# Sorted-block attention and a gated MLP on one core: six value loads issued in one row behind a softmax turn, one value product ahead of an output step, three copies on the other engine

## The chip, the cores and the metric

The kernel runs on one core of a Trainium2 chip. A core has five engines with instruction streams of their own: TensorE (PE in the profile; PEld is its weight load), VectorE (DVE), ScalarE (ACT), GpSimd (POOL) and SyncE (SP). Each runs its own stream in the order in which it was written, and they wait for each other, and for DMAs, on semaphores. The metric is the device time of one execution in microseconds (us); less is better.

## The reference

What is computed, cut to what matters (4 batches, 8 heads, 768 tokens, 64 wide; 8 blocks of 96 tokens; model width 512, inner width 2048):

```python
for _ in range(5):                          # P = sort_net, 8x8 for each head
    P = exp(P - max(P, -1)); P = P / (sum(P, -1) + 1e-9); P = P / (sum(P, -2) + 1e-9)
k_sorted = einsum('bhij,bhjcd->bhicd', P, k_b)      # blocks of keys mixed
v_sorted = einsum('bhij,bhjcd->bhicd', P, v_b)      # blocks of values mixed
scores = scale * q_b @ k_sorted^T                   # block by block, 96 x 96
attn = softmax(scores)
x = attn @ v_sorted                                  # as 3072 tokens x 512
h = x @ w_in                                         # 512 -> 2048
out = (h * cos(h)) @ w_out                           # 2048 -> 512
```

## The kernel before, in words

The work goes in eight **chunks** of 384 tokens: chunk n is half of the blocks (four of eight) of batch n // 2. Batches 0 and 1 are pair 0, batches 2 and 3 are pair 1. A chunk has four **turns** u, one for each block of 96 tokens:

- scores for all 8 heads on PE (`sc`), row maximum and subtraction on DVE (`qk_reduce`, lines 507 and 509), exp on ACT into one of three buffers `p_buf` (`expo`, line 587);
- the transpose of p, either by a DMA from SP's queue (line 607) or on PE (`p_ps`, line 854, with a copy `p_ev`);
- the **value product** (`av_products`, line 643), whose result DVE normalizes (`av_norm`, lines 654 and 656);
- the transpose of the normalized block into `xT`, by a DMA from SP's queue (line 662) or on PE with a copy out (`xp` and `xe`, lines 966 and 972).

The MLP of a chunk follows its attention: eight **up** steps (`uh`, line 915, with cosine on ACT, `uc`, and the product on DVE, `ug`), then three **output** blocks of 128 tokens, each in four quarters of four matmuls (`dn`, line 1012), copied out by `dc` (ACT for the first two blocks, DVE for the last) and stored.

Interleaved with it, the blocks of keys and values of the next pair are mixed: "key sort" (`kg`, `bt(('ks', ..))`, `sort_eight`) reads the tile `pair`, "value sort" (`vg`, `bt(('vs', ..))`) reads `vperm`. POOL makes `vperm` from `vbuf`, a half of the tile `kv`, by four large copies (`v_permute`, line 187). `vbuf` is loaded with pair 1's values by six loads (`load_pair`, line 101), each 128 rows by 1024 columns, from POOL's queue.

What sets the order is the code itself: the kernel turns the automatic schedule off, and the calls stand one behind the other by hand (lines 1028 to 1561). Each engine runs its share of them in that order. PSUM comes from two pools: `big` with three buffers of two banks (scores, value products, up steps, sorts), `acc` with two (output blocks, transposes). A new tile waits until the tile that had its buffer before has been read. The output tile of block (1,2) takes the `acc` buffer of block (1,1), so its first quarter, `dn(1, 2, 0)`, waits for the copy in `dc(1, 1)`.

Three more things matter for the change:

- `hold(t)` (line 615) is a tiny POOL copy out of a tile that a DMA writes. It has no use but to make POOL wait there: what POOL issues next is issued once that DMA has landed. `p_hold(n, u)` waits for the transposed p of turn u of chunk n.
- DMAs issued from POOL use eight semaphores in turn; each waits until the DMA eight places before it has landed. The eight loads of q for chunk 4 (`load_q(4)`) stand behind the six value loads, so the third to the eighth of them wait for the value loads, one each.
- SP's queue carries, in this order around the change: the two q transposes of chunk 3, the transposes of p of chunk 2 (turns 0, 1, 2), two stores, p of turn 0 of chunk 3, a store, the two q transposes of chunk 4, the two key swaps (`k_swap_b(0)`), p of turns 1 and 2 of chunk 3.

In the rows, L101 is `load_pair`, L138 is `load_q`, L158 `q_transpose_dma`, L265 and L267 the copy on ACT and on DVE.

Of the kernel before, what the change touches and what calls it, by code (L numbers as in the profile page):

```python
# [18 lines left out]
def kernel(  # L19
# [15 lines left out]
    nc = tc.nc  # L35
# [8 lines left out]
    CD = blk * D  # L44
# [24 lines left out]
    vbuf, kbuf = kv[:, :CD], kv[:, CD:]  # L69
# [24 lines left out]
    vin_d = v.rearrange("b h (j c) d -> b (h j) (c d)", j=nb)  # L94
# [4 lines left out]
    def load_pair(buf, src, lo, hi):  # L99

        nc.gpsimd.dma_start(  # L101
            out=buf[:, lo:hi], in_=src[2:4].rearrange("b r x -> (b r) x")[:, lo:hi])
# [158 lines left out]
    V, A = nc.vector, nc.scalar  # L261

    def copy_on(eng, dst, src):
        if eng is nc.scalar:
            eng.copy(dst, src)  # L265
        else:
            eng.tensor_copy(dst, src)  # L267
# [175 lines left out]
    def hold_keys():  # L443

        nc.gpsimd.tensor_copy(held[:], kT[1][:, 1, 0, :1])
# [70 lines left out]
    def by_half(n, u, sc):  # L516

        for h2 in range(H2):
            x = (u * H2 + h2) * blk
            for hp in range(2):  # L520
                rows = slice(hp * D, (hp + 1) * D)
                nc.tensor.matmul(  # L522
                    sc[:, hp, h2 * 128:h2 * 128 + blk], q_of(n, hp)[rows, x:x + 128],
                    keys_of(n, u, h2, hp)[rows], start=True, stop=True)

    def sort_eight(kind, z, ps):

        for t in range(8):
            for b in range(2):
                rows = slice(b * 64, (b + 1) * 64)  # L530
                if kind == "ks":
                    m, cols = 128, pair[rows, (z * 8 + t) * 2 * D:(z * 8 + t + 1) * 2 * D]
                else:
                    m, cols = 128, v_cols(z * 8 + t, True, 128)[rows]
                nc.tensor.matmul(
                    ps[:m, b, t * 2 * NB:(t + 1) * 2 * NB], cols,
                    bds[1][rows, b * H:(b + 1) * H].rearrange("p x i -> p (x i)"),
                    start=True, stop=True)
# [74 lines left out]
    def hold(t):  # L613

        nc.gpsimd.tensor_copy(held[:blk], t[:blk, 0, :1])

    def p_hold(n, u):
        hold(pT[n, u])
# [81 lines left out]
    def store(n, ts, o_s, eng=nc.sync):  # L700
        r0 = n * TC + ts * 128
        eng.dma_start(out=out[r0:r0 + 128, :], in_=o_s[:])
# [243 lines left out]
    def bt(*parts):  # L946
        for kind, *x in parts:
            o = big.tile([128, 2, 512], FP32, name=kind, tag="big")
            if kind == "sc":
                ps["q", x[0], x[1]] = o  # L950
                by_half(*x, o)
            else:
                ps["e", kind, x[0]] = o
                sort_eight(kind, x[0], o)

    def be(kind, z, eng):
        place_eight(kind, z, ps.pop(("e", kind, z)), eng)
# [11 lines left out]
    def xe(n, u, to, eng):  # L969
        hi = (u if to is None else to) + 1  # L970
        copy_on(eng, xT[n][:, :, u * blk:hi * blk],
                ps.pop(("t", n, u)).rearrange("p k i c -> p k (i c)"))
# [35 lines left out]
    def dn(n, ts, q):  # L1008
        if q == 0:
            out_ps[n, ts] = acc.tile([128, Dm], FP32, name="o", tag="acc")  # L1010
        for f in range(q * 4, q * 4 + 4):
            nc.tensor.matmul(  # L1012
                out_ps[n, ts][:], gt[n, q][:, f % 4, ts * 128:(ts + 1) * 128], w_out_t[:, f, :],
                start=(f == 0), stop=(f == FC - 1))

    def dc(n, ts, stores):
        if stores is None:
            z = (n % 2 * 3 + ts) * 2 * Dm
            o_s = vbuf[:, z:z + 2 * Dm].bitcast(FP32)
        else:  # L1020
            o_s = op.tile([128, Dm], FP32, name="o_s", tag="o_s")
        copy_on(V if ts == TC // 128 - 1 else A, o_s[:], out_ps.pop((n, ts))[:])
        if stores is None or stores == "held":
            kept[n, ts] = o_s
        else:
            store(n, ts, o_s, stores)
# [207 lines left out]
    zeros_between(3)  # L1234
    load_q(3)
    hold_keys()
    load_pair(vbuf, vin_d, 0 * CD // 6, 1 * CD // 6)
    load_pair(vbuf, vin_d, 1 * CD // 6, 2 * CD // 6)
    load_pair(vbuf, vin_d, 2 * CD // 6, 3 * CD // 6)
    uh(1, 0)  # L1240
    uc(1, 0)
    ug(1, 0)
# [61 lines left out]
    dn(1, 1, 1)  # L1304
    kg(16, *B)
    kge(16, A)
    dn(1, 1, 2)
    expo(2, 3, True)
    av_products(2, 0)
    av_norm(2, 0, True)  # L1310
    dn(1, 1, 3)
    dc(1, 1, nc.sync)
    bt(('sc', 3, 0), ('ks', 1, A))
    qr2(3, 0)
    be("ks", 1, A)
    p_hold(2, 2)
    load_pair(vbuf, vin_d, 3 * CD // 6, 4 * CD // 6)
    load_pair(vbuf, vin_d, 4 * CD // 6, 5 * CD // 6)
    load_pair(vbuf, vin_d, 5 * CD // 6, 6 * CD // 6)
# [12 lines left out]
    av_products(2, 2)  # L1332
    av_norm(2, 2, True)
    xp(2, 1, None, *B)
    xe(2, 1, None, V)
    av_products(2, 3)
    av_norm(2, 3, True)
    xp(2, 0, None, *C)
    xe(2, 0, None, V)
    dn(1, 2, 2)  # L1340
    kg(20, *B)
    kge(20, A)
# [61 lines left out]
    dn(2, 0, 3)  # L1404
    dc(2, 0, nc.sync)
    expo(3, 3)
    bt(('vs', 1, A), ('vs', 2, A))
    be("vs", 1, A)
    be("vs", 2, A)
    dn(2, 1, 0)  # L1410
    av_products(3, 0)
    av_norm(3, 0, False)
# [118 lines left out]
             None, mid={3: [(qk_av, 6, 1, 5, 2)]}, late=[(x_transpose, 5, 3, V, *B)])  # L1531
# [7 lines left out]
             None, mid={3: [(qk_av, 7, 1, 6, 2)]}, late=[(x_transpose, 6, 3, V, *B)])  # L1539
# [51 lines left out]
```

## Time and profile before

| what | value |
|---|---|
| time, median of 3 runs (lowest, highest) | 231.41 us (230.86, 231.49) |
| the profiled execution: time, span | 230.85 us, 229.1 us |
| TensorE clock granted | 1.0 |
| PE busy, of the span | 219.3 us (96%) |
| DVE, ACT, POOL busy | 171.8, 153.0, 95.2 us |
| PE busy from 69 to 84 us (15 us) | 14.69 us |
| PE busy from 96 to 110 us (14 us) | 13.48 us |

How to read the rows: a timeline row has the start in us from the span's start, the busy time in us, the engine, the line of the kernel, the operation, out<-in, the type, the count of instructions merged, and in brackets the idle time before them and what ended it. PE's matmuls are pipelined, so that rows of PE may overlap; the distance from start to start says more than their length. A DMA row ends with the count and the median time from issue to landing in us. The turns of chunk 2 lie between 70 and 84 us, those of chunk 3 between 97 and 110 us.

### The profile page before, as it was taken

To read this page: it belongs to the slowest core of one execution; us is meant where nothing else is said; L and a number is where in the kernel's file an instruction comes from. 1 tells how busy PE (TensorE), PEld (TensorE's weight loads), DVE (VectorE), ACT (ScalarE), POOL (GpSimd) and SP (SyncE) were. 2 spreads that over 40 slices of the span, in tenths; PEclk is the share of its full clock that TensorE was granted. 3 is DMA by queue.
4 is the path that set the end of the run, shared out by engine and by line. 5 is a ranking of instruction groups with operands and counts; after the bars stand their busy time and mean duration, and the time that the engine had idled before them with its cause. 6 is when DMAs were issued, how large, how long until landed. Compare 5 with 4: busy or idle time off the path is not lost.

```text
span 229.1 us, 5513 instructions
## 1 busy us (share of the span) xinstructions
PE 219.3 (96%) x2243; PEld 137.4 (60%) x2265; DVE 171.8 (75%) x297; ACT 153.0 (67%) x206; POOL 95.2 (42%) x120
## 2 busy tenths in 40 slices
PE   8688899999999999999999999999999999999994
PEld 3387798567665566645665456655655566555554
DVE  6779859987798768868589967987699769646700
ACT  5749865966989758897688466736674667716521
POOL 7999999299960288934517001800000000000000
PEclk9999999999999999999999999999999999999999
DMA  5999999996999699857979639953934440351012
GB/s 65 237 187 207 204 205 234 198 230 172 99 120 206 172 157 132 146 126 152 165 146 129 118 70 164 201 92 73 189 119 85 89 158 0 69 147 46 0 46 94
DMA packets 67833, 31.21 MB, mean 136 GB/s; under 512 B 56416, under 2 KB 63200, under 8 KB 67552
## 3 DMA queue, kind: packets, MB, share of 16 engines
q0 software_dynamic: 24048, 13.64, 43.4%
q1 hardware_dynamic: 43472, 17.02, 33.8%
q8 instruction: 18, 0.29, 0.6%
q10 hardware_dynamic: 288, 0.20, 0.3%
q14 instruction: 7, 0.06, 0.1%
HBM read 27.27 MB, written 6.29 MB: 147 GB/s over the span
## 4 chain that ended last, share of the span: by engine, by line
PE 80%; DVE 12%; ACT 4%; issue 2%; DMA 1%; ACTq 0%; DVEq 0%
PE h L687 18%; PE o L712 16%; PE h L915 14%; PE o L1012 11%; PE av L643 3%; DVE mx L839 3%; DVE s L843 3%; PE sc L457 3%; PE h L876 2%; PE ks L424 2%; PE o L897 2%; DVE gg L888 2%; PE o L1555 2%; ACT p_buf L587 1%; PE xps L966 1%
## 5 line engine op out<-in xcount | busy, mean ns | idle before, releaser
L687 PE MATMUL h<-xT,w_in_t 128*128 128x384 bf16 x256 | 43.2, 327 | 0.0
L691 ACT ACTIVATE c<-h,half_pi 128x768 f32<-128x768 f32 x32 | 28.8, 900 | 17.7 <-PE h L687 17.7
L712 PE MATMUL o<-w_out_t,gg 128*128 128x512 bf16 x169 | 39.9, 379 | 0.4
L695 DVE TENSOR_TENSOR gg<-c,h 128x768 bf16<-128x768 f32 x32 | 29.9, 950 | 11.6 <-ACT c L691 11.6
L915 PE MATMUL h<-xT,w_in_t 128*128 128x384 bf16 x192 | 35.2, 327 | 0.1
L687 PEld LDWEIGHTS <-w_in_t 128*128 128x128 bf16 x256 | 24.7, 98 | 16.2
L1012 PE MATMUL o<-w_out_t,gg 128*128 128x512 bf16 x134 | 33.7, 379 | 0.6 <-issue 0.3
L187 POOL COPY vperm<-kv 64x768 bf16<-64x768 bf16 (+2 forms) x12 | 28.4, 2417 | 4.8 <-DMA kv<-in_v_dram 4.8
L587 ACT ACTIVATE p_buf<-s 96x768 bf16<-96x768 f32 x32 | 26.6, 843 | 4.5 <-DVE s L509 4.0
L927 DVE TENSOR_TENSOR gg<-c,h 128x768 bf16<-128x768 f32 x24 | 22.7, 948 | 7.6 <-ACT c L921 7.6
L921 ACT ACTIVATE c<-h,half_pi 128x768 f32<-128x768 f32 x24 | 21.6, 900 | 8.3 <-PE h L915 7.4
L712 PEld LDWEIGHTS <-gg 128*128 128x128 bf16 x176 | 16.0, 98 | 16.5
L509 DVE TENSOR_TENSOR s<-sc,mx 96x384 f32<-96x384 f32 (+1 forms) x33 | 24.3, 735 | 1.6
L507 DVE TENSOR_REDUCE mx<-sc 96x4 f32<-96x384 f32 (+1 forms) x33 | 24.0, 728 | 0.4 <-PE sc L522 0.4
L915 PEld LDWEIGHTS <-w_in_t 128*128 128x128 bf16 x192 | 17.5, 98 | 9.9 <-DVE xT L267 0.3
L656 DVE TENSOR_TENSOR xn<-av,r 96x512 bf16<-96x512 f32 x32 | 22.0, 686 | 1.1
L1012 PEld LDWEIGHTS <-gg 128*128 128x128 bf16 x144 | 12.6, 97 | 12.0
L138 POOL DMA_DIRECT2D kv<-in_q_dram x24 | 16.0, 676 | 0.8 <-issue 0.8
L265 ACT COPY kv<-o 128x512 f32<-128x512 f32 (+2 forms) x10 | 5.2, 523 | 14.0 <-PE o L712 8.5
L265 ACT CAST kTs<-ks 128x512 bf16<-128x512 f32 (+1 forms) x17 | 10.4, 633 | 4.6 <-PE ks L424 4.6
L654 DVE RECIPROCAL r<-av 96x8 f32<-96x8 f32 x32 | 6.3, 197 | 7.3 <-PE av L643 7.1
L267 DVE COPY kv<-o 128x512 f32<-128x512 f32 (+1 forms) x5 | 3.1, 611 | 11.3 <-PE o L1555 8.5
(140 smaller groups left out, 335.9 us busy)
## 6 DMA issues: line engine op xcount, KB each, us to landing
out_dram<-kv SPq DMA_DIRECT2D x12, 256.0 KB, 2.7
out_dram<-o_s SPq DMA_DIRECT2D x10, 256.0 KB, 2.6
w_in_t<-in_moe_w_in_dram POOLq DMA_DIRECT2D x4, 512.0 KB, 12.0
w_out_t<-in_moe_w_out_dram POOLq DMA_DIRECT2D x4, 512.0 KB, 12.5
kv<-in_k_dram POOLq DMA_DIRECT2D x2, 768.0 KB, 10.3
kv<-in_v_dram POOLq DMA_DIRECT2D x2, 768.0 KB, 13.5
pair<-in_k_dram POOLq DMA_DIRECT2D x2, 768.0 KB, 13.2
kv<-in_v_dram POOLq DMA_DIRECT2D x6, 256.0 KB, 5.5
```

The source lines that it names most:

```text
L187: nc.gpsimd.tensor_copy(dst, src)
L507: nc.vector.reduce_max(mx[:], scv, axis=AX.X)
L509: nc.vector.tensor_tensor(s, scv, mx.to_broadcast(list(s.shape)), op=ALU.subtract)
L587: nc.scalar.activation(p[:, :, :blk], s_t.pop((n, u)).rearrange("p e h c -> p (e h) c"), AF.Exp, scale=scale)
L656: nc.vector.tensor_tensor(xn.rearrange("p h e d -> p e h d"), avv[:, :, :, :D], r.to_broadcast([blk, 2, H2, D]), op=ALU.mult)
L687: nc.tensor.matmul(h[:, f2, :w], w_in_t[:, kk, f * 128:(f + 1) * 128], xT[n][:, kk], start=(kk == 0), stop=(kk == KC - 1))
L691: nc.scalar.activation(c[:], h[:, :, :w], AF.Sin, bias=half_pi[:, 0:1])
L695: nc.vector.tensor_tensor(gt[n, fp // 2][:, f:f + 2], c[:], h[:, :, :w], op=ALU.mult)
L712: nc.tensor.matmul(o[:], gt[n, f // 4][:, f % 4, ts * 128:(ts + 1) * 128], w_out_t[:, f, :], start=(f == 0), stop=(f == FC - 1))
L915: nc.tensor.matmul(h[:, f2, :TC], w_in_t[:, kk, f * 128:(f + 1) * 128], xT[n][:, kk], start=(kk == 0), stop=(kk == KC - 1))
L927: nc.vector.tensor_tensor(gt[n, fp // 2][:, f:f + 2], ps.pop(("c", n, fp))[:], ps.pop(("h", n, fp))[:, :, :TC], op=ALU.mult)
L1012: nc.tensor.matmul(out_ps[n, ts][:], gt[n, q][:, f % 4, ts * 128:(ts + 1) * 128], w_out_t[:, f, :], start=(f == 0), stop=(f == FC - 1))
```

## The change

Three kinds of edits, no change to what is computed:

1. The first three of the six value loads leave their place behind `hold_keys()` and stand directly ahead of the other three. The wait ahead of these is now for p of turn 1 of chunk 2, and no longer for turn 2.
2. In the turns of chunk 2 the value product of turn 0 and its normalization stand ahead of the third quarter of output block (1,1), and the fourth quarter with its copy `dc(1, 1)` stands behind the scores of chunk 3, turn 0, and the key sort 1.
3. The copies `xe(2, 1)` and `xe(2, 0)` go from DVE to ACT; the eviction of value sort 2, `be("vs", 2, ..)`, goes from ACT to DVE.

```diff
     hold_keys()
-    load_pair(vbuf, vin_d, 0 * CD // 6, 1 * CD // 6)
-    load_pair(vbuf, vin_d, 1 * CD // 6, 2 * CD // 6)
-    load_pair(vbuf, vin_d, 2 * CD // 6, 3 * CD // 6)
     uh(1, 0)
...
     kge(16, A)
-    dn(1, 1, 2)
     expo(2, 3, True)
     av_products(2, 0)
     av_norm(2, 0, True)
-    dn(1, 1, 3)
-    dc(1, 1, nc.sync)
+    dn(1, 1, 2)
     bt(('sc', 3, 0), ('ks', 1, A))
     qr2(3, 0)
     be("ks", 1, A)
-    p_hold(2, 2)
+    dn(1, 1, 3)
+    dc(1, 1, nc.sync)
+    p_hold(2, 1)
+    load_pair(vbuf, vin_d, 0 * CD // 6, 1 * CD // 6)
+    load_pair(vbuf, vin_d, 1 * CD // 6, 2 * CD // 6)
+    load_pair(vbuf, vin_d, 2 * CD // 6, 3 * CD // 6)
     load_pair(vbuf, vin_d, 3 * CD // 6, 4 * CD // 6)
...
     xp(2, 1, None, *B)
-    xe(2, 1, None, V)
+    xe(2, 1, None, A)
...
     xp(2, 0, None, *C)
-    xe(2, 0, None, V)
+    xe(2, 0, None, A)
...
-    bt(('vs', 1, A), ('vs', 2, A))
+    bt(('vs', 1, A), ('vs', 2, V))
     be("vs", 1, A)
-    be("vs", 2, A)
+    be("vs", 2, V)
```

On POOL, from the q loads of chunk 3 on (`p_turned_138` is the transposed p of turn 2 of chunk 2, `p_turned_137` that of turn 1; L146 zeroes a part of `q_mem` for chunk 4):

```order
 L138 DMA kv<-in_q_dram 96x4x64 x8
 L445 CAST held<-kTs 128x1
-L101 DMA kv<-in_v_dram 128x1024 x3
 L146 MEMSET q_mem 96x16x64 x2
-L615 CAST held<-p_turned_138 96x1
-L101 DMA kv<-in_v_dram 128x1024 x3
+L615 CAST held<-p_turned_137 96x1
+L101 DMA kv<-in_v_dram 128x1024 x6
 L138 DMA q_mem<-in_q_dram 96x4x64 x8
 L187 COPY vperm<-kv 128x1536 x4
```

All six value loads now stand behind the wait for p of turn 1, and the q loads and the four permutes behind all six.

On ACT, in the turns of chunk 2, from the eviction of `kg(16)` to that of `kg(20)` (the `ks` of 8 columns is key sort 1, `o_s` is the copy of output block (1,1), `pps` the transposed p of turn 3):

```order
 L265 CAST kTs<-ks 128x2x2x32x4
 L587 ACTIVATE p_buf_105<-s 96x8x96
+L265 CAST kTs<-ks 128x2x2x32x8
 L265 COPY o_s<-o 128x512
-L265 CAST kTs<-ks 128x2x2x32x8
 L265 COPY p_turned_139<-pps 96x768
 L587 ACTIVATE p_buf_103<-s 96x8x96
+L265 COPY xT<-xps 128x4x96 x2
 L265 CAST kTs<-ks 128x2x2x32x4
```

The eviction of key sort 1 now stands ahead of the copy of the output block, and the two copies into `xT` are new on this engine.

## The prediction

> **What bounds the kernel now.** I read the page first, then the timeline of TensorE (PE) and of SyncE's DMA queue (SPq) from 63 to 84 us, then the waits, then the landing times of single DMAs.
>
> ```profile
> PE 219.3 (96%) x2243; PEld 137.4 (60%) x2265; DVE 171.8 (75%) x297; ACT 153.0 (67%) x206; POOL 95.2 (42%) x120
> ```
>
> PE bounds the kernel. An edit pays only where PE stands still, so the question is how much PE loses in the chunk-2 turns, and which wait ends last there. The timeline of PE (start, duration, line, count):
>
> ```profile
> 74.76 0.39 PE L424 MATMUL ks<-bd,pair 128*128 128x128 bf16 x4
> 74.98 1.03 PE L1012 MATMUL o<-w_out_t,gg 128*128 128x512 bf16 x4
> 76.01 0.42 PE L643 MATMUL av<-vS,p_turned 96*128 96x65 bf16 x8
> 76.27 1.03 PE L1012 MATMUL o<-w_out_t,gg 128*128 128x512 bf16 x4
> 77.23 0.34 PE L522 MATMUL sc<-kTs,q_turned 64*128 64x96 bf16 x8
> ...
> 77.74 0.42 PE L643 MATMUL av<-vS,p_turned 96*128 96x65 bf16 x8
> 77.99 0.50 PE L854 MATMUL pps<-ident,p_buf 96*128 96x96 bf16 x8
> 78.33 1.89 PE L1012 MATMUL o<-w_out_t,gg 128*128 128x512 bf16 x7
> 80.06 0.41 PE L643 MATMUL av<-vS,p_turned 96*128 96x65 bf16 x8
> 80.52 0.34 PE L966 MATMUL xps<-order,xn 96*128 96x96 bf16 x4
> ...
> 81.11 1.03 PE L1012 MATMUL o<-w_out_t,gg 128*128 128x512 bf16 x4
> 81.97 0.39 PE L424 MATMUL ks<-bd,pair 128*128 128x128 bf16 x4
> 82.20 0.73 PE L966 MATMUL xps<-order,xn 96*128 96x96 bf16 x8
> 82.76 0.81 PE L1012 MATMUL o<-w_out_t,gg 128*128 128x512 bf16 x3
> 83.63 0.49 PE L915 MATMUL h<-xT,w_in_t 128*128 128x384 bf16 x2
> ```
>
> From start to start the undisturbed groups take: a quarter output step (four matmuls) 0.86 (81.11 to 81.97), a value product 0.25 (77.74 to 77.99), the score with its key sort 0.51 (77.23 to 77.74), the p transposes 0.34 (77.99 to 78.33), two quarters 1.73 (78.33 to 80.06), a key sort 0.23 (81.97 to 82.20). Against these PE loses 0.17 at 74.98 (1.03 instead of 0.86), 0.10 at 76.27 (0.96), about 0.21 at 80.06 (0.46) and 0.22 at 82.20 (0.56 where eight transposes take 0.34). That is 0.70 us between 74.98 and 83.63, and all that this stretch can give. The busy share is a poor measure of it: the row at 74.98 "ends" at 76.01, where the next starts, and still hides 0.17. The Trainium skill says the same (Perfetto Trace Analysis, Identifying the Most-Contended Engine): matmul occupancy is no good measure, since pipelined matmuls overlap. By busy time there would be nothing to win at 76.01, by start-to-start 0.17; the trace agrees with the page.
>
> The 0.17 is a wait for a DMA:
>
> ```profile
> PEld L643 <- DMA p_turned<-p_buf: 0.5, 1, 0.5
> ...
> 65.11 6.71 SPq L158 DMA_TRANSPOSE q_turned<-kv  x2
> 71.92 4.78 SPq L607 DMA_TRANSPOSE p_turned<-p_buf  x3
> ...
> q_turned<-kv SPq DMA_TRANSPOSE x2, 7.8
> q_turned<-q_mem SPq DMA_TRANSPOSE x1, 4.0
> p_turned<-p_buf SPq DMA_TRANSPOSE x1, 4.0
> p_turned<-p_buf SPq DMA_TRANSPOSE x1, 2.9
> ```
>
> The last four rows are issue-to-landing times of single DMAs. The two transposes of q for chunk 3 (issued from 65.11, beside the first three value loads) take 7.8 on the mean and hold SPq for 6.71; the same pair at 91.70, with no value load under way, takes 4.0. They land by about 75. The first p of chunk 2, issued at 71.92, stands behind them: 4.0, landing at 75.9, where the p at 99.44 took 2.9.
>
> **The change, part by part.** *The first three value loads leave 63.46 and come behind p(2,1).* With them gone I expect the q transposes at 4.0, done by about 71, and p(2,0) at 71.92 + 2.9 = 74.8. Bounds: 2.9 (landing 74.8) and 4.0 (75.9); I take 2.9, because the q transposes' 7.8 against 4.0 is the only difference that the rows show.
>
> *The value product of turn 0 goes ahead of a quarter.* PE is free for it at 74.98. With p(2,0) at 74.8 it starts there and the 0.17 is gone; with p(2,0) at 75.9 it starts at 76.01 and PE stands still for 1.03, because the quarter that covered the wait is now queued behind it.
>
> *The quarter dn(1,1,3) goes behind the score and the key sort.* This moves its copy on ACT, and that costs. The two rows of ACT:
>
> ```profile
> 77.33 0.58 ACT L265 COPY o_s<-o 128x512 f32<-128x512 f32 x1 [0.44 <-PE o L1012]
> 77.85 1.01 ACT L265 CAST kTs<-ks 128x1024 bf16<-128x1024 f32 x1
> ```
>
> Now the copy is first, the key eviction second. In the new order the eviction is first. The acc pool has two buffers, and the output tile of the next row block, dn(1,2,0), takes the buffer that this copy frees. Worked through: product 74.98 to 75.23, quarter to 76.10, 0.10 as before, score and key sort 76.20 to 76.71, quarter dn(1,1,3) to 77.57, product to 77.82, p transposes to 78.16. The copy can start 1.06 after its quarter (76.27 to 77.33), so at 77.77, and the eviction (from about 76.85, 1.01 long) ends at 77.86 with 0.06 overlap: the copy runs 77.80 to 78.38, and PE resumes about 0.07 later, at 78.45. A new wait of 0.29 stands where none was. Bounds: 0 (the copy done by 78.16) and 0.4; I take 0.29.
>
> *Two of four xT copies go from DVE to ACT.* The two quarters then run 78.45 to 80.18. The subtract on DVE, on which the product's normalization waits, starts with the score (76.20 instead of 77.23), so the 0.21 before the first x transposes goes: product to 80.43, transposes, product, transposes to 81.02, quarter to 81.88, key sort to 82.11, transposes to 82.28. The last ones wait for the last xn:
>
> ```profile
> 81.35 0.34 DVE L267 COPY xT<-xps 128x384 bf16<-128x384 bf16 x1
> 81.84 0.69 DVE L656 TENSOR_TENSOR xn<-av,r 96x512 bf16<-96x512 f32 x1
> 83.89 0.69 DVE L267 COPY o_s<-o 128x512 f32<-128x512 f32 x1 [0.56 <-PE xps L966]
> ```
>
> The 0.34 copy before it is gone (0.26 net of overlap), the third product comes 0.12 later and xn 0.14: xn ends at 82.41 instead of 82.53. Last quarter from 82.64, chunk-2 up step at 83.51 instead of 83.63. ACT carries the two copies in the gap between its exp of turn (3,0) and its next key eviction; without that gap they would cost up to 0.34 each.
>
> *One value eviction goes from ACT to DVE at 101.* DVE copies 128x512 in 0.69, so 1024 columns in at most 1.4, with nothing behind it on DVE but the next normalization, which moves by about 0.2 and feeds a DMA transpose that has time. The wait there stays:
>
> ```profile
> 103.24 0.40 PE L643 MATMUL av<-vS,p_turned 96*128 96x65 bf16 x8 [0.15 <-ACT pair L265]
> ```
>
> It is for the buffer of the eviction before (vs 1), which stays on ACT. I cost this edit at 0, between -0.1 and +0.2.
>
> *The six value loads in one row.* POOL and the DMAs:
>
> ```profile
> 78.50 0.18 POOL L615 CAST held<-p_turned 96x1 f32<-96x1 bf16 x1 [11.55 <-DMA p_turned<-p_buf]
> 78.95 1.60 POOL L101 DMA_DIRECT2D kv<-in_v_dram  x3 [0.27 <-issue]
> ...
> 86.58 0.67 POOL L138 DMA_DIRECT2D q_mem<-in_q_dram  x1 [0.74 <-DMA kv<-in_v_dram]
> 87.25 11.26 POOL L187 COPY vperm<-kv 128x1536 bf16<-128x1536 bf16 x4
> ...
> kv<-in_v_dram POOLq DMA_DIRECT2D x1, 256.0 KB, 4.0
> kv<-in_v_dram POOLq DMA_DIRECT2D x1, 256.0 KB, 6.3
> kv<-p_buf SPq DMA_TRANSPOSE x1, 7.7
> ...
> 98.16 0.40 PE L535 MATMUL vs<-bd,vperm 64*128 64x64 bf16 x16
> ...
> 91.70 3.60 SPq L158 DMA_TRANSPOSE q_turned<-q_mem  x2
> ...
> 96.53 0.59 SPq L438 DMA_DIRECT2D kTs<-kTs  x1
> 99.44 1.47 SPq L607 DMA_TRANSPOSE p_turned<-p_buf  x1
> ```
>
> The first load of the three landed 4.0 after 78.95, the last 6.3 after 79.99: one per 1.68. p(2,1) should land near 76.05, so the loads start at 76.4 instead of 78.95, the first lands at 80.4, the sixth at 80.4 + 5 x 1.68 = 88.8 instead of 86.3. The last q load waits for it (row 86.58), so the permutes and the q transposes come 2.5 later: 89.8 and 94.2. The permutes (2.8 each) are first needed by the value sort at 98.16: hidden, 5 to spare. (If that cover were gone, each us of lateness would be one of PE.) SPq has 2.3 free before p(3,1) (97.12 to 99.44), and p(3,1), landing at 102.3, is wanted at 103.24: 3.2 in all against 2.5. Hidden, with 0.7 left. Spacings of 1.5 to 1.95 give a shift of 1.6 to 3.9, so a cost between 0 and 0.7.
>
> The sum: 83.63 to 83.51, and PE has no slack after it that could take the gain back or give more: **-0.12 us**. The profiled execution took 230.85 (span 229.1 and 1.75 around it); it becomes 230.73. It lies 0.56 under the median of 231.41, so against the runs shown I predict **231.3 us**, no change that can be told (within 0.3%, 0.7 us, is about what a measurement here can tell from none).
>
> **Rivals.** *A, the forecast*: -0.4 to +0.3.
>
> *B, p(2,0) still lands at 75.9.* Its 4.0 would then be its own or that of other traffic. PE starts the product at 76.01, every later step slides, and the up step starts at 84.50: +0.87, 232.3. It decides from a landing of about 75.1 on. For it: the margin is 0.15 us. Against it: the 2.9 row, and a cause that the rows show.
>
> *C, all losses go.* The copy on ACT is done in time and xn as well: up to the whole 0.70 and the 0.3 at 103.24, so -0.4 to -1.0, 230.4 to 231.0. For it: ACT's order is tight by only 0.3. Against: xn's chain on DVE has no room.
>
> *D, the loads hit the transposes.* p(3,0) took 7.7 beside three value loads. If the shift of 2.5 is 3.9, or p(3,1) lands late behind the key swaps, the product at 103.24 slips by 0.4 to 0.7; if p(2,2), issued near 74.9, took 7.7 beside the first new load, it would land at 82.6 and cost 2.3. Time 231.8 to 233.6. Against: p(2,2) has 2.4 of slack and is issued ahead of the loads. The Trainium skill (DMA: Bandwidth & Descriptors, Queues, rings and completion order) says that each DMA engine takes turns between its queues packet by packet; by that, p(2,2) shares the engines with the loads from their first packet, whoever came first, and the row of 7.7 agrees.
>
> **How the numbers follow.** A 0.50, C 0.20, B 0.14, D 0.16. Faster by over 0.3%: most of C and a little of A's scatter, 0.20. Slower: B, and D's larger half, 0.22. The rest 0.58. The likeliest one's own range is 230.9 to 231.7; with B, C and the small end of D it reaches 230.4 to 232.4.
>
> **What would show it.** Right: q transposes of chunk 3 landing in about 4, p(2,0) in about 2.9, the value product right behind the key sort at 75, a new wait of PE for ACT's o_s copy at 78.2, the up step near 83.5. Wrong: the product of turn 0 waiting for its DMA (B); no wait at 78.2 (C); a wait for p at 80 or 103 (D).

## The result, and the profile after

The changed kernel takes **232.73 us** (median of 4 runs, 232.38 to 233.02), the kernel before 231.13 (4 runs, 230.84 to 231.49): the ratio is **1.0068, 95% interval 1.0042 to 1.0093**. It is slower by 1.6 us, where 231.3 and "no change that can be told" was forecast and the range ended at 232.4. The profiled execution took 232.38, its span is 230.5 (before 230.85 and 229.1): 1.4 us more. Of the runs further down one, of loads_only (235.59), fell in a slower state of the chip, and its ratio leaves that run out.

Where they came in is read from the start of the first up step of each chunk in PE's timeline. The distance from one to the next is called a **stage** from here on; "stage 2" ends with chunk 2's first up step and holds the turns of chunk 2.

| stage (us) | before | after | difference |
|---|---|---|---|
| start of chunk 0's up steps | 26.11 | 26.10 | -0.01 |
| 1 | 29.55 | 29.55 | 0.00 |
| 2 | 27.97 | 28.66 | **+0.69** |
| 3 | 26.78 | 27.21 | **+0.43** |
| 4, 5, 6 | 25.29, 23.30, 23.31 | 25.29, 23.31, 23.31 | +0.01 |
| 7 | 22.59 | 22.90 | **+0.31** |

So there are three losses, in three places, and one of them is far from everything that the change touches. The timeline of PE in stage 2, after (start, duration, line; in brackets the idle time and what ended it):

```profile
74.76 0.39 PE L424 MATMUL ks<-bd,pair 128*128 128x128 bf16 x4
75.85 0.42 PE L643 MATMUL av<-vS,p_turned 96*128 96x65 bf16 x8 [0.70 <-DMA p_turned<-p_buf]
...
78.69 0.50 PE L854 MATMUL pps<-ident,p_buf 96*128 96x96 bf16 x8
79.28 1.89 PE L1012 MATMUL o<-w_out_t,gg 128*128 128x512 bf16 x8
81.01 0.41 PE L643 MATMUL av<-vS,p_turned 96*128 96x65 bf16 x8
...
84.31 0.65 PE L915 MATMUL h<-xT,w_in_t 128*128 128x384 bf16 x3
```

The value product of turn 0 does not follow the key sort at 74.98, it starts at 75.85: PE loses 0.87 and waits for the DMA of p. The second loss, 0.25 ahead of 79.28, is the one that the prediction expected for ACT's copy. The timeline of SyncE's queue, after, and the landing time of the first p:

```profile
65.01 3.64 SPq L158 DMA_TRANSPOSE q_turned<-kv  x2
71.91 4.62 SPq L607 DMA_TRANSPOSE p_turned<-p_buf  x3
```

```profile
p_turned<-p_buf SPq DMA_TRANSPOSE x1, 3.9
```

The first row is what step 1 hoped for: without the value loads the two q transposes hold the queue for 3.64 and no longer for 6.71. The last row is what it did not expect: p(2,0), issued at 71.91, still takes 3.9. The cause that the prediction named is gone, and the lateness has stayed.

What the DMA engines did meanwhile stands in the view of DMA traffic, 72 to 76 us in 40 slices of 0.1 us, after:

```profile
GB/s 0 0 0 0 0 0 0 0 164 0 15 120 156 156 154 143 174 210 136 28 0 8 10 8 10 10 8 10 51 274 274 34 113 164 164 159 177 164 223 276
...
q1 hardware_dynamic: 1371, 0.34, 80.6%
q8 instruction: 1, 0.02, 2.0%
```

Nothing moves until 72.8. There stands one packet of 16 KB (164 GB/s in 0.1 us) of the queue that the profile calls "q8 instruction"; it took 1.25 us of one engine (2.0%, rounded, of 16 engines in 4 us). From 73.1 to 73.9 the transpose runs at some 160 GB/s. Then, for 0.8 us, 8 to 10 GB/s are left: a sixteenth of 160, which is what one engine alone would move. They begin at 74.1, when the packet is through. The same trickle stands in the kernel before from 74.2 to 75.0, behind a packet at 73.2, where a quarter of an output step covered it (72 to 76 us, before):

```profile
GB/s 289 210 123 284 289 292 289 287 289 287 292 274 339 154 169 141 161 195 205 118 8 0 5 5 10 10 8 10 10 10 141 284 178 54 156 164 159 184 146 174
```

### The profile page after: what moved, and what is told of

It is laid out like the page before. It is cut to its first block, busy times and chain, and to the rows that moved or that the text cites. A ratio compares the mean times of both kernels' runs of the same rounds, so it can differ in the third digit from the quotient of the medians.

```text
span 230.5 us, 5537 instructions
## 1 busy us (share of the span) xinstructions
PE 221.0 (96%) x2265; PEld 137.2 (60%) x2265; DVE 172.6 (75%) x296; ACT 153.1 (66%) x207; POOL 95.4 (41%) x120
## 4 chain that ended last, share of the span: by engine, by line
PE 80%; DVE 8%; DMA 5%; ACT 4%; issue 1%; ACTq 0%
PE h L687 18%; PE o L712 15%; PE h L915 14%; PE o L1012 10%; PE o L897 4%; PE av L643 3%; DMA p_turned<-p_buf 3%; PE sc L457 3%; PE h L876 3%; PE ks L424 2%; PE o L1555 2%; DVE mx L839 2%; DMA xT<-xn 1%; DVE s L843 1%; DVE gg L888 1%
## 5 line engine op out<-in xcount | busy, mean ns | idle before, releaser
L712 PE MATMUL o<-w_out_t,gg 128*128 128x512 bf16 x176 | 41.1, 379 | 0.0
L1012 PE MATMUL o<-w_out_t,gg 128*128 128x512 bf16 x144 | 34.9, 379 | 0.1
L138 POOL DMA_DIRECT2D q_mem<-in_q_dram x16 | 10.8, 683 | 6.3 <-DMA kv<-in_v_dram 6.0
L897 PE MATMUL o<-w_out_t,gg 128*128 128x512 bf16 x48 | 11.8, 379 | 0.0
```

The costliest lines, as they stand in the source:

```text
L138: nc.gpsimd.dma_start(out=q_heads[:, i, :, e], in_=src[:, ih * IC + i, :, e])
L712: nc.tensor.matmul(o[:], gt[n, f // 4][:, f % 4, ts * 128:(ts + 1) * 128], w_out_t[:, f, :], start=(f == 0), stop=(f == FC - 1))
L1012: nc.tensor.matmul(out_ps[n, ts][:], gt[n, q][:, f % 4, ts * 128:(ts + 1) * 128], w_out_t[:, f, :], start=(f == 0), stop=(f == FC - 1))
```

## Experiments

In the table are the stages of all kernels that ran, from one profiled execution each, with the landing time of p(2,0) and the time against the kernel before (ratio, 95% interval).

| kernel | p(2,0) lands in | start | stage 1 | 2 | 3 | 4 to 6 | 7 | ratio |
|---|---|---|---|---|---|---|---|---|
| before | 4.0 | 26.11 | 29.55 | 27.97 | 26.78 | 71.90 | 22.59 | 1 |
| after | 3.9 | 26.10 | 29.55 | 28.66 | 27.21 | 71.91 | 22.90 | 1.0068 (1.0042 to 1.0093) |
| order_only | 3.7 | 26.22 | 29.55 | 28.73 | 26.78 | 71.91 | 23.16 | 1.0071 (1.0059 to 1.0083) |
| loads_only | 4.1 | 26.18 | 29.55 | 28.06 | 29.64 | 71.90 | 22.60 | 1.0067 (1.0043 to 1.0090) |
| copies_only | 4.0 | 26.09 | 29.55 | 28.03 | 26.77 | 71.91 | 22.92 | 1.0007 (0.9997 to 1.0016) |
| shift_after | 2.8 | 26.69 | 29.54 | 27.79 | 27.73 | 71.90 | 23.29 | 1.0090 (1.0077 to 1.0103) |
| shift_before | 4.0 | 26.54 | 29.54 | 28.11 | 26.88 | 72.22 | 23.33 | 1.0084 (1.0071 to 1.0098) |
| fill_after | 2.8 | 26.30 | 29.55 | 27.78 | 27.54 | 72.24 | 23.31 | 1.0078 (1.0064 to 1.0092) |
| fewer_after | 2.8 | 27.75 | 29.54 | 27.79 | 27.67 | 72.03 | 22.93 | 1.0121 (1.0083 to 1.0158) |
| dc_kept_after | 3.8 | 26.14 | 29.55 | 28.40 | 27.33 | 71.90 | 22.91 | 1.0062 (1.0048 to 1.0076) |
| q_first_after | 3.7 | 26.10 | 29.54 | 28.45 | 27.56 | 71.97 | 23.10 | 1.0066 (1.0051 to 1.0082) |
| swap_first_after | 3.6 | 26.10 | 29.55 | 28.41 | 27.62 | 71.91 | 22.91 | 1.0076 (1.0058 to 1.0094) |
| pad_after | 4.1 | 26.08 | 29.54 | 28.89 | 28.00 | 71.90 | 22.59 | 1.0059 (1.0039 to 1.0079) |
| best2 | 2.9 | 26.29 | 29.55 | 27.58 | 27.81 | 72.09 | 23.60 | 1.0096 (1.0066 to 1.0126) |
| best3 | 2.8 | 27.69 | 30.71 | 27.58 | 27.28 | 71.91 | 22.59 | 1.0103 (1.0073 to 1.0133) |

### The parts alone: order_only, loads_only, copies_only

The order alone is the kernel before with

```diff
-    dn(1, 1, 2)
     expo(2, 3, True)
     av_products(2, 0)
     av_norm(2, 0, True)
-    dn(1, 1, 3)
-    dc(1, 1, nc.sync)
+    dn(1, 1, 2)
     bt(('sc', 3, 0), ('ks', 1, A))
     qr2(3, 0)
     be("ks", 1, A)
+    dn(1, 1, 3)
+    dc(1, 1, nc.sync)
```

> The kernel before with one part of the change alone: the value product of turn 0 goes ahead of the quarter dn(1,1,2), and dn(1,1,3) with its way out behind the key sort. The value loads and the copies stay. In the trace of the changed kernel the product started at 75.85 after a wait of PE, and the chunk-2 up step 0.68 late. Theory 1 (the order costs this, since p(2,0) lands at 75.9 in both kernels): product at 75.9 to 76.0, up step 0.7 to 0.9 late, the product of turn 2 of chunk 3 no later than that, time +0.7 to +0.9 us (ratio 1.003 to 1.004). Theory 2 (the loads in one row cost everything, the order alone nothing): ratio 0.999 to 1.001, up step at 83.6.

The loads alone:

```diff
     hold_keys()
-    load_pair(vbuf, vin_d, 0 * CD // 6, 1 * CD // 6)
-    load_pair(vbuf, vin_d, 1 * CD // 6, 2 * CD // 6)
-    load_pair(vbuf, vin_d, 2 * CD // 6, 3 * CD // 6)
...
-    p_hold(2, 2)
+    p_hold(2, 1)
+    load_pair(vbuf, vin_d, 0 * CD // 6, 1 * CD // 6)
+    load_pair(vbuf, vin_d, 1 * CD // 6, 2 * CD // 6)
+    load_pair(vbuf, vin_d, 2 * CD // 6, 3 * CD // 6)
```

> The kernel before with the other part alone: the first three value loads leave their place at 63 us and stand behind the wait for p(2,1), in one row with the other three. Theory 1: the up step of chunk 2 stays at 83.6 (the quarter covers p(2,0), wherever that lands by 75.9), and the last loads, the q transposes behind them and p(3,1) come late, so the first product of chunk 3 slips by 0.2 to 0.5: time +0.3 to +0.5 us (1.001 to 1.002). Theory 2 (all of the loss comes from the loads): +1.0 to +1.4 us (1.004 to 1.006). The prediction's own step 1: p(2,0) lands at 74.8 once the loads are gone, the 0.17 before the product vanishes, and chunk 3 pays nothing: -0.2 us.

The three copies alone (the hunks with `xe` and `vs` of the change):

> The kernel before with only the three copies on the other engine: two xT copies of chunk 2 from DVE to ACT, the eviction of vs 2 from ACT to DVE. The prediction's steps 3 and 4: from the up step of chunk 1 to that of chunk 2 0.1 us less (27.88 instead of 27.98), from there to chunk 3's the same 26.78 or up to 0.2 less, since the third value product of chunk 3 waits 0.15 for ACT; time -0.1 to -0.3 us, ratio 0.9985 to 1.000. Rival: the copies are part of the loss, because ACT, which carries them, is late with its next key eviction: +0.2 us or more, ratio above 1.001.

Rows of PE's timeline; order_only, then loads_only, then copies_only:

```profile
75.77 0.42 PE L643 MATMUL av<-vS,p_turned 96*128 96x65 bf16 x8 [0.50 <-DMA p_turned<-p_buf]
...
84.50 0.49 PE L915 MATMUL h<-xT,w_in_t 128*128 128x384 bf16 x2
```

```profile
106.24 0.42 PE L643 MATMUL av<-vS,p_turned 96*128 96x65 bf16 x8 [3.00 <-DMA p_turned<-p_buf]
```

```profile
76.28 0.42 PE L643 MATMUL av<-vS,p_turned 96*128 96x65 bf16 x8 [0.28 <-DMA p_turned<-p_buf]
...
82.47 0.51 PE L966 MATMUL xps<-order,xn 96*128 96x96 bf16 x8
82.81 0.81 PE L1012 MATMUL o<-w_out_t,gg 128*128 128x512 bf16 x3
83.67 1.46 PE L915 MATMUL h<-xT,w_in_t 128*128 128x384 bf16 x8
```

The order costs 0.76 in stage 2 and nothing in stage 3, as theory 1 had it. The loads cost nothing that matters in stage 2 (0.09) and all of theirs in stage 3: in this execution 2.86, where 0.2 to 0.5 was expected. It took 233.89, 1.6 above the median (232.26) and the most of the six runs that its ratio rests on (231.57 to 233.89), so this size is one of the larger ones. In loads_only the q transposes of chunk 3 have no value load beside them (they land in 4.0 and 4.4), and p(2,0) still takes 4.1: **the value loads are not what makes it late.** The copies cost nothing up to the last stage (27.97 to 28.03, 26.78 to 26.77). Stage 7, which none of the parts touches, is 0.3 to 0.6 longer with the order or the copies. The three parts cost 0.7, 0.7 and 0.1% alone and 0.7% together: the losses do not add up, so what follows looks at one stage at a time.

### Moving the packet of PE's program: shift_after, shift_before, fill_after, fewer_after

The page of the changed kernel counts 18 packets of 16 KB on q8, and 2265 matmuls and 2265 weight loads of PE: about one packet per 250 instructions. Three edits move it without touching the work. The first, on both kernels, makes PE's program 106 instructions longer in the warm-up at the start:

```diff
-    keep_warm(14, big.tile([128, 512], FP32, name="idle", tag="big"))
+    idle = big.tile([128, 512], FP32, name="idle", tag="big")
+    keep_warm(64, idle, 64)
+    keep_warm(3, idle)
```

> The changed kernel with 53 more matmuls in the warm-up at the start: 64 matmuls of 64 columns and 3 of 512 in place of 14 of 512, while PE waits for the first q anyway. They do nothing but lengthen PE's program by about 106 instructions, so that the 16 KB packets of the eighth DMA queue, which come once per 256 instructions of PE, come about 106 instructions earlier: the one at 72.9 moves to about 70. Theory F (that packet sits on one DMA engine for 1.25 us while p(2,0) is written, and makes it land after 3.9 instead of 2.9): p(2,0) lands in 2.8 to 3.1 from 71.9, the value product starts at 75.0 without a wait for it, the up step comes 0.5 to 0.8 earlier than in the changed kernel, time -0.5 to -0.8 us against it, so +0.4 to +0.8 against the kernel before (1.002 to 1.0035). Theory G (the 3.9 are p(2,0)'s own, as the first of three transposes in a row): nothing moves, 3.9, product at 75.85, ratio 1.006 to 1.008.

> The kernel before with the same 53 more matmuls in the warm-up. Theory F: p(2,0) lands before 75.2 instead of 75.9, unless the q transposes of chunk 3, which share the engines until 73.3, are what then ends last; the wait of 0.17 behind the quarter at 74.98 goes: -0.1 to -0.2 us, ratio 0.999 to 1.000. Theory G and the prediction's own (the value loads, by way of the q transposes): p(2,0) still takes 4.0, nothing moves.

The second makes it 48 longer in gaps of PE between 21 and 24 us:

```diff
-    p_ps(0, 1, *C, fill=2)
+    p_ps(0, 1, *C, fill=2, more=6)         # more: matmuls of 48 columns
...
-    av_products(0, 1, fill=2)
+    av_products(0, 1, fill=8, cols=48)     # 8 of 48 columns in place of 2 of 256
...
-    av_products(0, 0)
+    av_products(0, 0, fill=12, cols=48)
```

> The changed kernel with 24 small matmuls more in gaps of PE between 21 and 24 us, where it waits for ACT (6 of 48 columns, 8 of 48 in place of 2 of 256, 12 of 48): 48 instructions of PE more, with no time of their own. The packet of PE's program that came at 72.9 should come at about 71. Theory F (that packet makes p(2,0) land after 3.9): p(2,0) in 2.8 to 3.1, no wait ahead of the value product, from the up step of chunk 1 to that of chunk 2 27.8 instead of 28.66, time -0.6 to -0.9 us against the changed kernel: ratio 1.002 to 1.0045 to the kernel before. Theory G (p(2,0)'s own): 28.66 and 1.006 to 1.008.

The third makes it 24 shorter, so that the packet comes behind the transpose:

```diff
-    keep_warm(14, big.tile([128, 512], FP32, name="idle", tag="big"))
+    keep_warm(10, big.tile([128, 512], FP32, name="idle", tag="big"))
...
-            idle(4)
+            idle(3)
...
-            idle(2)
+            idle(1)
...
-            idle(2)
+            idle(1)
...
-    v0(6, *C, fill=1)
+    v0(6, *C)
...
-    p_ps(0, 1, *C, fill=2)
+    p_ps(0, 1, *C)
...
-    p_ps(0, 0, *B, fill=2)
+    p_ps(0, 0, *B, fill=1)
...
-    av_products(0, 1, fill=2)
+    av_products(0, 1, fill=1)
```

> The changed kernel with 12 warm-up matmuls less before 23 us (10 in place of 14 at the start, three fewer between the first q transposes, five fewer among the value products of chunk 0): PE's program is 24 instructions shorter, and since PE issues only two instructions per 0.215 us in the quarters at 71 to 75, the packet at 72.9 should come 2.4 us later, at 75.3. Theory F: p(2,0) then lands in 2.8 to 3.1, no wait for it, stage of chunk 2 27.8 (changed kernel 28.66) - this time with the packet behind the transpose, where the two earlier kernels had it ahead. Theory G (in those two, the extra matmuls or the later issue at 72.1 to 72.5 did it): 3.9 and 28.6. If PE is colder for it, the loss shows before 26 us.

The packet moved from 72.8 to 70.3 in shift_after, to 72.1 in fill_after, and to 78.0 in fewer_after, where all of stage 2 begins 1.64 later. In all three p(2,0) lands in 2.8 and stage 2 shrinks from 28.66 to 27.78 or 27.79. Rows of SyncE's queue and of PE in fewer_after:

```profile
73.55 4.10 SPq L607 DMA_TRANSPOSE p_turned<-p_buf  x3
...
76.40 0.39 PE L424 MATMUL ks<-bd,pair 128*128 128x128 bf16 x4
76.62 0.41 PE L643 MATMUL av<-vS,p_turned 96*128 96x65 bf16 x8
```

and its DMA traffic from 73.6 to 77.6 us, in slices of 0.1:

```profile
GB/s 0 0 0 0 0 0 0 0 0 0 0 77 161 169 151 172 169 202 269 276 195 108 18 0 26 115 156 174 166 136 189 218 284 241 162 87 13 0 0 0
```

No packet, no trickle: the first transpose is through in 1.1 us (74.7 to 75.8), and the product follows the key sort at once. p is issued here as far behind the stage's start as in the changed kernel (73.55 - 57.29 = 16.26; 71.91 - 55.65 = 16.26), so its issue is not what changed. Theory F holds, G falls. The packet has not lost its effect at its new place: at 78.0 it falls on p(2,2), which lands in 4.2 where it took 2.9 or 3.0, but nothing waits for that one. shift_before did not move what it was meant to move: with the value loads in their old place the packet came at 72.8, while the q transposes still kept the engines busy (until 73.3), and p(2,0) took 4.0 as before. So it tells nothing for or against F. All four edits cost something elsewhere, so that none is faster: 53 matmuls more at the start lost 0.43 to 0.59 by 26 us, most of it in a wait of PE at 14.6 that the profile puts down to PE's own key sort; 12 fewer lost 1.65 there, which is the clock (the stretch of 13 to 16 us in fewer_after, where 60 matmuls ran; the three numbers at the end are granted clock, DMA share and GB/s; the changed kernel has 93 matmuls there and a clock of 1.00):

```profile
13.00:16.00 3.00, 3.00 (x60) 2.98 (x58) 1.92 (x6) 0.58 (x1) 2.78 (x3) 0.50 1.17 193
```

Of its six runs the one with a clock of 0.999 took 231.94, the five with 0.971 or 0.985 took 233.69 to 235.30.

### The copy behind the key eviction: dc_kept_after

```diff
     dn(1, 1, 2)
+    dn(1, 1, 3)
+    dc(1, 1, nc.sync)
     bt(('sc', 3, 0), ('ks', 1, A))
     qr2(3, 0)
     be("ks", 1, A)
-    dn(1, 1, 3)
-    dc(1, 1, nc.sync)
```

> The changed kernel with the last quarter of row block 1 and its way out, dn(1,1,3) and dc(1,1), back ahead of the score and key sort; the value product stays ahead of the third quarter. The prediction's step 2 (the copy behind the key eviction costs PE a wait for the acc buffer, 0.25 in the trace of the changed kernel at 79.28): that wait goes, the up step of chunk 2 comes 0.2 to 0.3 earlier (28.4 instead of 28.66), ratio 1.0050 to 1.0062. Rival: the wait moves to the key tiles or to the next product: 28.66, and the ratio of the changed kernel.

The transposes of p at 78.67 are followed by the quarters at 79.02, 0.35 later, which is their own 0.34: the wait is gone, and stage 2 is 0.26 shorter (28.40). Step 2 of the prediction is confirmed with its size. The time, 1.0062 against 1.0068, cannot tell so little.

### Stage 3: q_first_after, swap_first_after

In q_first_after `load_q(4)` stands ahead of the six value loads.

> The changed kernel with the eight q loads of chunk 4 ahead of the six value loads instead of behind them. Theory D (chunk 3 loses 0.43 because the q loads stand behind six value loads, so that the q transposes start 2.9 late, SyncE's queue reaches p(3,1) 0.84 late, and p(3,1) then lands behind PE): the q transposes of chunk 4 go right behind SyncE's earlier work at about 84 to 88, p(3,1) is issued within 0.2 of its exp, no wait of PE for p in chunk 3, up step to up step 26.8 instead of 27.21, time -0.4 us against the changed kernel (ratio 1.0045 to 1.0055 to the kernel before). Rival (the value loads themselves are late for the permutes, and these for the value sort): the permutes begin at 95 or later, PE waits for vperm, and the stage grows beyond 27.2.

In swap_first_after `q_transpose_dma(4)` stands behind `k_swap_b(0)`.

> The changed kernel with the two q transposes of chunk 4 behind the two key swaps on SyncE's queue instead of ahead of them. So far p(3,1) landed in 2.8 to 2.9 where it was issued 0.7 us or more behind the last key swap (the kernel before, the copies alone), and in 3.8 to 4.0 where it came right behind it (the changed kernel, and three variants of it). Theory D2 (the swap just ahead is what makes p(3,1) land late): the swaps go at about 93 to 95, the q transposes up to 99, p(3,1) lands in 2.8 to 3.0, PE waits for no p at 104, up step to up step of chunk 3 26.8 to 26.95 instead of 27.21, time -0.3 to -0.4 us against the changed kernel. Rival (SyncE's queue is simply late, whatever stands last in it): p(3,1) is issued at 100.2 or later behind the q transposes, takes 3.8, 27.2.

Rows of POOL and of PE in q_first_after:

```profile
96.40 2.85 POOL L187 COPY vperm<-kv 128x1536 bf16<-128x1536 bf16 x1 [9.74 <-DMA kv<-in_v_dram]
...
99.30 0.41 PE L535 MATMUL vs<-bd,vperm 64*128 64x64 bf16 x16 [0.52 <-POOL vperm L187]
...
104.48 0.41 PE L643 MATMUL av<-vS,p_turned 96*128 96x65 bf16 x8
```

With the q loads first, PE waits for no p in chunk 3 (104.48 has no wait), as theory D has it. But the rival comes true beside it: the permutes begin at 96.40 (92.06 in the changed kernel) and the value sort waits for them, 0.52 and 0.27, so that stage 3 is longer, 27.56. The cover that hides the permutes has an end, and here it was reached. Theory D2 fell: with the swaps gone from ahead of it, p(3,1) stood behind the q transposes instead, was issued at 100.65 and took the same 3.8, with a wait of PE of 0.99. So it is not the swap as such: with another transfer of SyncE's queue directly ahead the landing is as late. A packet of PE's program at 100.2 falls on these transposes too, so this run does not show the queue's share by itself.

### Stage 7: pad_after

```diff
+    for _ in range(8):
+        nc.vector.memset(idle_d[:], 0.0)          # in a gap of DVE at 30 us
     gate_four(0, 0)
...
+    for _ in range(8):
+        nc.scalar.copy(idle_a[:], half_pi[:])     # in a gap of ACT at 38 us
     cos_four(1, 1)
```

> The changed kernel with eight tiny copies more on ACT ahead of 40 us and eight tiny memsets more on DVE ahead of 31 us, in gaps where each waits. In every run so far the last stage (up step of the last block less that of the one before) takes 22.59 where the one packet of the fourteenth queue near 204 comes 2.2 us behind the issue of the third x transpose, and 22.9 to 23.2 where it comes 1.6 to 1.85 behind it. Theory P (that packet, of another engine's program, sits on one DMA engine while the transpose is written): eight instructions earlier it comes some us sooner, the transpose lands in 2.3, the last stage takes 22.6, -0.3 us. Rival (the last stage is late for another reason, and the packet only marks it): 22.9, wherever the packet goes. If the packet is of SyncE's or POOL's program, it stays at 204.7 and the run tells nothing.

The packet of the fourteenth queue went from 204.8 to 200.8, and stage 7 takes 22.59, as in the kernel before. The chain of waits, changed kernel first, pad_after second:

```profile
202.93 3.27 DMA xT<-xn
206.20 0.14 issue
206.33 4.71 PE h L687 x28
```

```profile
206.30 0.86 PE o L712 x4
207.16 2.93 PE h L687 x18
```

In the changed kernel the last stage's up steps waited for an x transpose of 3.27; in pad_after, as before, PE comes from its own work. Theory P holds in this execution and in that of best3 further down, which has the same pads (packet at 201.5, stage 7 22.59). What is late shows in the packets: in the changed kernel the transpose's data are through by 204.75, and of the 32 packets of 4 bytes behind them 30 come by 204.95 and two at 205.3, when the fourteenth queue's packet of 8 KB (204.84, 0.46 us) is over; the kernel before has all 32 ahead of its packet. (Stages 2 and 3 of this execution were longer than the changed kernel's, 28.89 and 28.00; the median of its times is 232.14.) The packet moved by instructions on ACT and DVE, so it is of one of their programs; which of the two was not tried.

### Mended versions: best2, best3

best2 is the changed kernel with the edits of fill_after, dc_kept_after and swap_first_after.

> The changed kernel with three things mended: 24 small matmuls more in PE's gaps at 21 to 24 us (the packet of PE's program passes before p(2,0) is written), dn(1,1,3) and dc(1,1) back ahead of the score and key sort, the q transposes of chunk 4 behind the key swaps. By theories F, D2 and step 2: chunk 1's up step to chunk 2's 27.5 (before: 27.98), to chunk 3's 26.8 to 27.0 (before: 26.78), the rest as in the changed kernel, with 0.3 to 0.7 lost in the last stage: ratio 0.999 to 1.002 to the kernel before. By the prediction's own step 1 (value loads alone): no gain over the changed kernel but step 2's 0.25, 1.005 to 1.006.

best3 is the kernel before, its loads untouched, with the order of dc_kept_after, the three copies, the shorter warm-up of fewer_after and the pads.

> The kernel before with the parts of the change that the runs so far leave standing, and none of the loads: the value product ahead of the quarters dn(1,1,2) and dn(1,1,3) with dc(1,1) behind them and ahead of the score, the three copies, 12 warm-up matmuls less (the packet of PE's program behind p(2,0)), eight tiny instructions more on ACT and on DVE (the packet near 204 ahead of the last x transposes). By theories F and P: chunk 2's stage 27.5 to 27.6 (before 27.98), chunk 3's 26.8, the last 22.6: -0.3 to -0.5 us, ratio 0.998 to 0.9987. If the q transposes of chunk 3, slowed by the value loads to 73.3, hold p(2,0) back by themselves: chunk 2's stage 28.2 to 28.5, ratio 1.001 to 1.002.

Rows of best3: SyncE's queue, the landing times of the q transposes and of p(2,0), then PE.

```profile
66.42 6.80 SPq L158 DMA_TRANSPOSE q_turned<-kv  x2
74.65 4.10 SPq L607 DMA_TRANSPOSE p_turned<-p_buf  x3
```

```profile
q_turned<-kv SPq DMA_TRANSPOSE x1, 7.4
p_turned<-p_buf SPq DMA_TRANSPOSE x1, 2.8
```

```profile
77.51 0.39 PE L424 MATMUL ks<-bd,pair 128*128 128x128 bf16 x4
77.73 0.41 PE L643 MATMUL av<-vS,p_turned 96*128 96x65 bf16 x8
```

The value loads are in their old place, the q transposes take 7.4 and hold the queue for 6.80, about as before, and p(2,0) lands in 2.8. It is issued 1.1 us further behind them than in the kernel before, though, so that their data end at 74.7, before its own begin at 75.8. That slow q transposes just ahead would cost p(2,0) nothing is therefore not shown here; that they are not needed for its lateness loads_only has shown. In both, stage 2 takes 27.58, 0.39 less than before: so much is this order, with dc(1, 1) ahead of the score, worth when the packet is elsewhere. Both are slower all the same. best2 loses 1.03 in stage 3 (p(3,1) behind the q transposes) and 1.01 in stage 7 (a packet of PE's program at 202.8 falls on an x transpose there, which takes 4.7 instead of 2.3), best3 1.58 before its first up step and 1.16 in stage 1, where PE ran colder (granted clock 0.50 from 26.7 to 30.1 us), and 0.50 in stage 3. No version here beats the kernel before.

## Why the prediction was wrong

**PE bounds the kernel, and the terms are read start to start: right.** Each loss showed as idle time of PE, and the unit durations held (in the changed kernel a value product 0.25, a quarter 0.87).

**Step 1, p(2,0) in 2.9 without the value loads: wrong, and the step that failed.** The working took "the only difference that the rows show" for the cause. The q transposes did come down (4.4 at most instead of 7.8), p(2,0) did not (3.9). What the prediction had not looked at is the packet of PE's own program at 72.8 in the DMA traffic; the kernel before has it too, at 73.2, and there a quarter of an output step covers its 1 us but for 0.17. The change took that cover away: that is the 0.87 at 74.98. Three kernels without the packet at that place show 2.8 and no wait, and loads_only shows 4.1 with the packet and without the value loads. The rest of the sum for stage 2 held. The up step came at 84.31, 0.80 behind the forecast 83.51; of that, 0.87 is this term, and all the others together gave 0.07 back. The Trainium skill (DMA: Bandwidth & Descriptors, Queues, rings and completion order), which the prediction named for the loads, says that an engine drains a whole packet before it takes one of another queue; the trickle of one sixteenth of the rate behind a packet of 1.25 us agrees. The Trainium skill also says (Runtime: NRT & Kernel Launch, Instruction fetch mechanics) that programs are fetched in blocks of 256 instructions over DMA queues and that this is mostly hidden. The blocks agree with the 18 packets; "mostly hidden" does not hold for a transpose that PE waits for, and the measured 0.87 decides.

**Step 2, a new wait for ACT's copy: right.** Forecast 0.29 at 78.16; it stands at 79.03, 0.25 long, since all is 0.87 later. ACT's rows have the order that was foretold:

```profile
77.68 1.01 ACT L265 CAST kTs<-ks 128x1024 bf16<-128x1024 f32 x1 [0.95 <-PE ks L535]
78.64 0.59 ACT L265 COPY o_s<-o 128x512 f32<-128x512 f32 x1
```

**Steps 3 and 4, the copies: right.** From the value product of turn 2 to the up step the changed kernel takes 3.30 (81.01 to 84.31), where 3.33 was forecast (80.18 to 83.51) and the kernel before takes 3.57. In copies_only the last x transposes take their own 0.34 (82.47 to 82.81), where the kernel before lost 0.22 there. That gain did not reach the end of stage 2, because p(2,0) was issued 0.28 later and PE waited for it. The eviction on DVE cost nothing (26.77 against 26.78).

**Step 5, the loads hidden with 0.7 to spare: the shift was nearly right, the landing of p(3,1) wrong, and rival D came true beside B.** Rows of POOL and of SyncE's queue, after:

```profile
77.00 0.18 POOL L615 CAST held<-p_turned 96x1 f32<-96x1 bf16 x1 [11.87 <-DMA p_turned<-p_buf]
77.48 3.23 POOL L101 DMA_DIRECT2D kv<-in_v_dram  x6 [0.29 <-issue]
...
91.39 0.67 POOL L138 DMA_DIRECT2D q_mem<-in_q_dram  x1 [2.15 <-DMA kv<-in_v_dram]
92.06 8.47 POOL L187 COPY vperm<-kv 128x1536 bf16<-128x1536 bf16 x3
...
94.64 3.63 SPq L158 DMA_TRANSPOSE q_turned<-q_mem  x2
98.37 1.16 SPq L437 DMA_DIRECT2D kTs<-kTs  x1
99.59 0.59 SPq L438 DMA_DIRECT2D kTs<-kTs  x1
100.28 3.49 SPq L607 DMA_TRANSPOSE p_turned<-p_buf  x2
```

The loads began at 77.48, not at 76.4, because p(2,1) stands behind p(2,0) and landed at 76.9, not at 76.05; the last q load went at 91.39, the permutes at 92.06 (forecast 89.8), the q transposes at 94.64 (forecast 94.2, before 91.70). The queue lost 2.94 where 2.5 was forecast, which the 3.2 of the sum would still have hidden. p(3,1) went 0.84 late, but 0.68 of that is the shift of stage 2 and only 0.16 the queue's. What the sum did not hold is the place: p(3,1) went directly behind the key swaps, and its data moved only behind theirs (DMA traffic in slices of 0.1 us; after from 100 us, before from 99.2 us):

```profile
GB/s 93 310 215 154 0 276 184 154 276 31 184 277 31 400 369 399 338 307 31 31 0 31 0 74 189 189 179 148 164 205 220 159 269 244 49 0 0 33 146 159
```

```profile
GB/s 0 0 0 164 0 0 0 0 0 0 0 0 0 0 77 177 151 161 159 184 200 264 248 187 116 41 3 0 0 3 100 166 177 146 161 187 212 276 266 180
```

Before, the transpose issued at 99.44 begins to move at 100.6, 1.2 later; after, the one issued at 100.28 at 102.3, 2.0 later, behind a stretch of faster traffic. It lands in 3.8 instead of 2.9. A packet of PE's program stands here too. Before (the 164), it is over when the transpose moves and does no harm. After, it begins at 100.18 and takes 1.12 while the key swaps move, and these end in single packets of 3 KB (the 31s from 101.8 on) until the transpose begins: the sign of one late engine again. So this trace does not part the two causes. shift_after does: no packet of PE's program falls between 95.6 and 106.1 there, and p(3,1), issued at 100.42 directly behind the swaps, still takes 3.7, and PE waits for it:

```profile
104.12 0.42 PE L645 MATMUL av<-vS,p_turned 96*128 96x65 bf16 x8 [0.65 <-DMA p_turned<-p_buf]
```

The place behind the swaps is enough to make it late; how much of the changed kernel's 0.43 the packet adds is not shown. PE of the changed kernel:

```profile
104.08 0.42 PE L643 MATMUL av<-vS,p_turned 96*128 96x65 bf16 x8 [0.31 <-DMA p_turned<-p_buf]
104.33 1.03 PE L1012 MATMUL o<-w_out_t,gg 128*128 128x512 bf16 x4
105.45 0.41 PE L643 MATMUL av<-vS,p_turned 96*128 96x65 bf16 x8
```

The product at 104.08 is 0.16 later than the shift of stage 2 explains, the next one 0.27 more (1.37 behind it instead of 1.10), since p(3,2), behind p(3,1) in the queue, was issued at 102.56 instead of 101.01: 0.43, within the 0.4 to 0.7 that D had named. In the profiled executions of all kernels with the loads in one row stage 3 was between 0.43 and 2.86 longer than before.

**Stage 7, +0.31: no step and no rival had it.** It is a packet again, of another engine's program, on the last x transpose, which takes 3.27 instead of 2.3.

**The rivals.** B (+0.87, given 0.14) and D (0.16) were weighed as alternatives to the forecast and to each other. They happened together: stage 2 is 0.69 longer, stage 3 0.43. B, which decides the sign, was set low because the working had one explanation for the 4.0 that fitted its rows, and took that for the only one. C, the gain, was there in part: with the packet moved, the change's own order takes 27.78 in stage 2, 0.19 less than before, and the order of best2 and best3 27.58, 0.39 less.

**What stays open.** How the 0.43 of stage 3 divides between the place behind the key swaps and the packet; why the packet in stage 7 comes 1.9 us behind the issue of the x transpose in the changed kernel, order_only and copies_only, and 2.2 behind it in the kernel before and loads_only; what PE waits for at 14.6 us in shift_after and shift_before; and why loads_only spreads from 231.57 to 233.89.

## What to carry to other kernels

A wait on a DMA that work now covers has a price only when the cover goes: before an edit takes away the cover, look at what that DMA's engines carry at that moment, programs among it, and not only at what is queued ahead of it. A DMA transpose that lands 1 us late at one place and not at its like elsewhere is worth a look at the traffic in slices of 0.1 us; one sixteenth of the rate for a while was here the sign that one engine was late. And a small gain won by moving a few instructions can be lost far behind the edit, where another packet falls on another transfer (copies_only lost 0.33 in stage 7), so compare by stages first and by the total last.

## What the runs showed that was not expected

- A packet of 16 KB of PE's program, about one per 250 instructions, held one of 16 DMA engines for 1.25 us; a transpose that is written then landed in 3.6 to 4.1 us instead of 2.8 to 2.9.
- Where such a packet falls depends on how many instructions an engine has, so 24 matmuls in a gap at 21 us changed the time of a stage at 75 us by 0.88, and eight tiny instructions each on ACT and DVE at 30 to 40 us that of one at 206 us by 0.31.
- Twelve warm-up matmuls fewer of 29 in the first 23 us left the granted clock at 0.50 from 13 to 16 us and cost 1.65 us.
